# Attention and a gated feed-forward in one kernel: the softmax division moved behind the value product, the sigmoid made of exp and reciprocal, and the step order written anew

## The chip, the core and the metric

The kernel runs on one core of a Trainium2 chip. A core has a matrix engine (PE, with its weight loads shown as PEld), a vector engine (DVE), a scalar engine (ACT), a general engine (POOL) and a queue engine (SP) that issues most DMAs. Each engine takes its instructions in order; engines wait for each other by semaphores. The metric is the device time of one execution in microseconds.

## The reference

Attention of 4 batches, 8 heads, 768 positions and 64 features, in which a query sees only the keys that share its 6-bit hash; its output is the input of a gated feed-forward. All arrays are float32.

```python
q_bits = (np.einsum('bhsd,dk->bhsk', q, proj) > 0)     # same for k
mask = q_bucket[:, :, :, None] == k_bucket[:, :, None, :]
scores = np.where(mask, scale * np.matmul(q, k.transpose(0, 1, 3, 2)), -1e9)
attn = np.exp(scores - np.max(scores, axis=-1, keepdims=True))
attn = attn / (np.sum(attn, axis=-1, keepdims=True) + 1e-09)
x = np.matmul(attn, v)            # heads laid side by side: (4, 768, 512)
gate_pre = sum(conv_w[k] * xp[:, k:k + S, :] for k in range(5))   # causal
gate = 1.0 / (1.0 + np.exp(-gate_pre))
out = (gate * (x @ w_val)) @ w_out
```

## The kernel before

A *unit* is one batch and head (32 in all); a *tile* is 128 query rows of a unit, so a unit has six tiles and the program 192 steps `k`. In the words below, `r` is `k % 6`. Products that need float32 accuracy are made of float32r parts: a high part and a remainder, `aq`/`bq` for the queries, `ak`/`bk` for the keys, `xh`/`xl` for the attention output, `hh`/`hl` for the gated values, two halves of each weight.

The order of PE, ACT, DVE and POOL is the order in which the Python code issues instructions (`manual_schedule`); SP's is set by a scheduler. One step of the loop issues:

- `keep_transposed`: two ACT copies of a transposed tile from PSUM (`tp`) to `pt`;
- `maxima`, `factors`, `shifts`: DVE takes the row maximum `nm` of the scores, then two tiny operations give `gs` and `nb`;
- `row_sums`, `recip`, `normalise`: DVE adds 1e-9 to the row sums of two tiles, takes their reciprocal `ri`, and POOL multiplies each tile `p` (128x768) by it;
- `scores` of the next tile: four PE matmuls into `s` (two PSUM buffers, so tile k+2 waits for the exponential of tile k);
- `exponentials`: ACT makes `p` from `s` and sums its rows (`sm`);
- a step of `convs`: generator `pair_x`, which for each pair of heads makes `xh`, `xl` and the five-tap gate `g` (DVE, 128x768);
- steps of `weights`: converting the float64-stored weights, one every unit or so, until about the tenth unit;
- a step of `moes`: the feed-forward of a finished batch. A *chunk* is a value product (`val`) or an output product (`outp`), 12 matmuls cut into *thirds* of 4; a batch has 8 + 6 chunks. All of them accumulate in one PSUM buffer `m` until the loop is over;
- a step of `preps`: the parts `aq`, `bq`, `ak`, `bk` of the next unit, made with DVE, POOL and six SBUF-to-SBUF DMAs;
- two steps of `avs` on odd `k`: `attn_v`, the value product of a unit, six key blocks of four matmul records each into `av`;
- `transposes` of tile k-3 (`LAG = 3`): six PE transposes into `tp` (two buffers).

A value product ends with two ACT copies of `av` into `x`. When the last pair of a batch has its gate, ACT makes all four sigmoids, for which it loads another table and then the exponential's again; only then does the batch's feed-forward begin. Two output products of each batch but the last are held back until the next batch's feed-forward is there. After the loop, the rest of the feed-forward runs with five PSUM buffers.

## Time and profile before

| | us |
|---|---|
| median of three runs (637.18 to 638.35) | 637.83 |
| the profiled execution, its own time | 637.56 |
| its span in the trace | 635.6 |
| first row maximum starts | 11.5 |
| row maximum of step 48 starts (first batch done) | 148.1 |
| row maximum of step 191 (the last) starts | 575.7 |

The span falls into a head of 11.5 us, a first batch of steps 0 to 47 in which there is no feed-forward but the weights are converted, steps 48 to 191 in which the feed-forward of the batch before runs between the attention's matmuls, and a tail in which the last batch's feed-forward is left. In the rows of the profile, a busy PE is one that has a matmul in flight; how long a group of matmuls holds PE is read from the start of one group to the start of the next.

### The profile page before, as it was taken

Reading aid. Unit: us, or ns where it says so; the run is one execution under the profiler, and the core shown is the slowest. Engines: PE = TensorE matmul, PEld = TensorE weight load, DVE = VectorE, ACT = ScalarE, POOL = GpSimd, SP = SyncE. Lnnn points to the kernel's source line nnn. Section 1 sums busy time; section 2 is a strip of 40 time slices with the busy share of each in tenths; the row PEclk is TensorE's granted clock in tenths of the full one; section 3 lists DMA queues with packets and bytes.
Section 4 is the critical chain, followed back from the end, with each engine's and each line's share of the span. In section 5 each row is a group of like instructions: output and inputs, shape, how many; then the busy total and the mean of one; then the engine's idle time right before and its main releaser. Section 6 shows DMA issues by size and latency. Waiting matters only on the chain.

```text
span 635.6 us, 10630 instructions
## 1 busy us (share of the span) xinstructions
PE 590.1 (93%) x3496; PEld 424.3 (67%) x3496; DVE 465.9 (73%) x1064; ACT 421.7 (66%) x881; POOL 364.7 (57%) x326
## 2 busy tenths in 40 slices
PE   4689888878999999999999999999999999999997
PEld 2465554555567777676667877677667777776895
DVE  5789897999986766668675877578685787665532
ACT  3487776767778666667787766677778677675400
POOL 1375868577765764567653776466562677544221
PEclk9899998998999999999999999999999999999999
DMA  6533535443332334343433333343422223300111
GB/s 243 128 101 86 139 96 138 112 134 81 104 80 58 83 75 123 82 105 96 104 80 79 88 80 110 80 121 80 120 57 61 57 53 79 86 18 2 50 51 50
DMA packets 23269, 56.76 MB, mean 89 GB/s; under 512 B 4296, under 2 KB 4296, under 8 KB 23216
## 3 DMA queue, kind: packets, MB, share of 16 engines
q1 hardware_dynamic: 23072, 56.06, 32.9%
q8 instruction: 28, 0.46, 0.3%
q14 instruction: 25, 0.20, 0.1%
q10 hardware_dynamic: 144, 0.03, 0.0%
HBM read 23.12 MB, written 6.29 MB: 46 GB/s over the span
## 4 chain that ended last, share of the span: by engine, by line
PE 64%; DVE 18%; ACT 10%; issue 3%; DMA 3%; POOL 0%; DVEq 0%; ACTq 0%
PE av L303 16%; PE s L232 15%; PE tp L280 12%; PE m L390 8%; PE m L365 7%; DVE nm L238 6%; ACT p L256 4%; DVE g L334 3%; ACT pt L289 3%; ACT x L311 2%; DMA w<-in_w_out_dram 2%; DVE aq L166 1%; PE tp L365 1%; PE tp L390 1%; PE s L390 1%
## 5 line engine op out<-in xcount | busy, mean ns | idle before, releaser
L271 POOL TENSOR_SCALAR p<-p,ri 128x768 f32<-128x768 f32 x192 | 220.0, 1150 | 200.3 <-DVE nb L248 157.6
L256 ACT ACTIVATE p<-s,nb,gs 128x768 f32<-128x768 f32 x192 | 192.7, 1004 | 49.7 <-DVE nb L248 44.6
L289 ACT COPY pt<-tp 128x384 f32<-128x384 f32 x384 | 166.2, 485 | 86.0 <-PE tp L280 85.0
L238 DVE TENSOR_REDUCE nm<-s 128x1 f32<-128x768 f32 x192 | 182.4, 950 | 52.8 <-PE s L232 52.6
L280 PEld LDWEIGHTS tp<-ident,p 128*128 128x128 f32 x1152 | 130.4, 142 | 74.2 <-issue 47.3
L280 PE MATMUL tp<-ident,p 128*128 128x128 f32 x1152 | 165.4, 280 | 4.5 <-ACT pt L289 1.6
L232 PE MATMUL s<-ak,aq 76*128 76x384 f32 x384 | 118.6, 390 | 32.2 <-ACT p L256 25.4
L303 PE MATMUL av<-pt,vt 128*64 128x384 f32 x768 | 146.9, 504 | 0.0
L232 PE MATMUL s<-bk,bq 128*128 128x384 f32 x384 | 101.6, 346 | 0.0
L232 PEld LDWEIGHTS s<-ak,aq 76*128 76x128 f32 x384 | 59.4, 195 | 48.9 <-ACT p L256 39.3
L303 PEld LDWEIGHTS av<-pt,vt 128*64 128x64 f32 x768 | 47.4, 137 | 63.3 <-issue 62.7
L334 DVE SCALAR_TENSOR_TENSOR g<-x,cw_sb,g 128x768 f32<-128x768 f32 x64 | 78.4, 1225 | 0.2
L232 PEld LDWEIGHTS s<-bk,bq 128*128 128x128 f32 x384 | 71.9, 194 | 0.5 <-issue 0.5
L376 POOL TENSOR_TENSOR hl<-ht,hh 128x384 fp32r<-128x384 f32 x32 | 33.4, 1044 | 45.5 <-DVE hh L374 45.5
L168 POOL TENSOR_TENSOR bq<-r,aq 128x768 fp32r<-128x768 f32 x31 | 58.4, 1885 | 0.5 <-DVE aq L166 0.5
L311 ACT COPY x<-av 64x384 f32<-64x384 f32 x64 | 30.4, 475 | 33.5 <-PE av L303 32.9
L365 PE MATMUL m<-xh,wv 128*128 128x384 f32 x200 | 42.7, 337 | 0.0
L248 DVE TENSOR_SCALAR nb<-nm,gs 128x1 f32<-128x1 f32 x192 | 40.1, 209 | 3.5
L370 DVE TENSOR_TENSOR ht<-m,g 128x384 f32<-128x384 f32 x25 | 13.9, 555 | 35.4 <-PE m L365 32.0
L256 ACT ACTIVATION_READ_ACCUMULATOR p<-s,nb,gs 128x1 f32 x192 | 39.1, 204 | 0.0
L324 POOL TENSOR_TENSOR xl<-x,xh 128x384 fp32r<-128x384 f32 x32 | 33.5, 1066 | 9.5 <-DVE xh L323 9.5
L390 PE MATMUL m<-wo,hh 128*128 128x512 f32 x144 | 38.1, 394 | 0.0
(84 smaller groups left out, 475.6 us busy)
## 6 DMA issues: line engine op xcount, KB each, us to landing
r<-in_qk_dram SPq DMA_DIRECT2D x32, 384.0 KB
vt<-in_v_dram SPq DMA_DIRECT2D x16, 384.0 KB
out_dram<-o SPq DMA_DIRECT2D x24, 256.0 KB
ak<-aq SPq DMA_DIRECT2D x31, 192.0 KB
bk<-aq SPq DMA_DIRECT2D x31, 192.0 KB
bk<-bq SPq DMA_DIRECT2D x31, 192.0 KB
bq<-aq SPq DMA_DIRECT2D x31, 192.0 KB
w<-in_w_val_dram SPq DMA_DIRECT2D x4, 512.0 KB
```

Of the source, the lines that this page charges most:

```text
L168: nc.gpsimd.tensor_tensor(out=bq, in0=r, in1=aq.bitcast(FP32), op=ALU.subtract)
L232: nc.tensor.matmul(out=s[:, hf, 0:HS], lhsT=lq[0:n, qs], rhs=rk[0:n, hf * HS:(hf + 1) * HS], start=n == M, stop=n == P)
L238: nc.vector.tensor_reduce(out=nm, in_=s[:, :, 0:HS], axis=AX.XY, op=ALU.max, negate=True)
L256: nc.scalar.activation(out=p, in_=s[:, :, 0:HS], func=AF.Exp, bias=nb, scale=gs.pop(k), accum_out=sm[:, k % 2, 0:1])
L271: nc.gpsimd.tensor_scalar(out=p, in0=p, scalar1=rcs.pop(k), scalar2=1.0, op0=ALU.mult, op1=ALU.mult)
L280: nc.tensor.transpose(out=tp[:, n * P:(n + 1) * P], in_=p[:, kb * P:(kb + 1) * P], identity=ident)
L289: nc.scalar.copy(out=pt[:, :, qo:qo + P], in_=tp[:, 0:HS].rearrange("p (a b) -> p a b", b=P))
L303: nc.tensor.matmul(out=av[s * D:(s + 1) * D, 0:HS], lhsT=vt[:, kb, hh * D:(hh + 1) * D], rhs=pt[kb // 3][:, kb % 3, :], start=(kb == 0), s ...
L311: nc.scalar.copy(out=x[hh * D:(hh + 1) * D, o:o + HS], in_=av[s * D:(s + 1) * D, 0:HS])
L334: nc.vector.scalar_tensor_tensor(out=g, in0=x[:, k:k + S], scalar=w, in1=g, op0=ALU.mult, op1=ALU.add)
L365: nc.tensor.matmul(out=acc[:, 0:HS], lhsT=wv[wi][:, c, j * P:(j + 1) * P], rhs=xs_[(c, o)][xi], start=(m == 0), stop=(m == 11))
L390: nc.tensor.matmul(out=acc, lhsT=hs[(o, j)][hi][:, tb * P:(tb + 1) * P], rhs=wo[wi][:, j, :], start=(m == 0), stop=(m == 11))
```

## The change

The diff is cut to what sets the order and the costs.

```diff
-    LAG = 3
+    LAG = 1
...
+    rp = ctx.enter_context(tc.tile_pool(name="rp", bufs=2))
+    dp = ctx.enter_context(tc.tile_pool(name="dp", bufs=2, space=bass.MemoryType.DRAM))
...
-        nc.vector.tensor_copy(out=aq, in_=r)
+        nc.gpsimd.tensor_copy(out=aq, in_=r)
...
-    def normalise(k):
-        p, _ = ps[k]
-        nc.gpsimd.tensor_scalar(out=p, in0=p, scalar1=rcs.pop(k), scalar2=1.0, op0=ALU.mult, op1=ALU.mult)
+    def row_sums(i):
+        s1 = small.tile([P, KB], FP32, name="s1", bufs=2)
+        nc.vector.tensor_scalar(out=s1, in0=sms.pop(i), scalar1=1e-9, scalar2=None, op0=ALU.add)
+        ri = small.tile([P, KB], FP32, name="ri", bufs=2)
+        nc.vector.reciprocal(out=ri, in_=s1)
+        rows = dp.tile([2, P, KB // 2], FP32, name="rows")
+        nc.sync.dma_start(out=rows.rearrange("s p t -> p s t"), in_=ri.rearrange("p (s t) -> p s t", s=2))
+        return rows
+
+    def row_factors(i, rows):
+        rb = rbs[i] = rp.tile([P, P, KB // 2], FP32, name="rb")
+        for s in range(2):
+            nc.sync.dma_start(out=rb[s * D:(s + 1) * D], in_=rows[s].partition_broadcast(D))
...
+    def take(i, av):
...
-            nc.scalar.copy(out=x[hh * D:(hh + 1) * D, o:o + HS], in_=av[s * D:(s + 1) * D, 0:HS])
+            nc.vector.tensor_tensor(out=x[hh * D:(hh + 1) * D, o:o + HS].rearrange("d (t p) -> d t p", p=P),
+                                    in0=av[s * D:(s + 1) * D, 0:HS].rearrange("d (t p) -> d t p", p=P),
+                                    in1=rb[s * D:(s + 1) * D].rearrange("d p t -> d t p"), op=ALU.mult)
...
-            nc.vector.tensor_copy(out=xh, in_=x0)
+            nc.gpsimd.tensor_copy(out=xh, in_=x0)
...
+        if c == NP - 1:
+            moes.append(moe(b, xs_, gs))
...
-            for g in gs:
-                nc.scalar.activation(out=g, in_=g, func=AF.Sigmoid)
+        nc.scalar.activation(out=g, in_=g, func=AF.Exp, scale=-1.0)
+        yield
+        nc.gpsimd.tensor_scalar(out=g, in0=g, scalar1=1.0, scalar2=3.0e38, op0=ALU.add, op1=ALU.min)
+        yield
+        nc.vector.reciprocal(out=g, in_=g)
+        yield
...
-                nc.vector.tensor_copy(out=hh, in_=ht)
+                nc.gpsimd.tensor_copy(out=hh, in_=ht)
...
+            puts.append(lambda: put(o + tb * P, acc))
+        def put(r0, acc):
             ob = op.tile([P, 512], FP32, name="o")
-            if cur["gates"]:
-                nc.vector.tensor_copy(out=ob, in_=acc)
-            else:
-                nc.scalar.copy(out=ob, in_=acc)
+            nc.scalar.copy(out=ob, in_=acc)
...
+    def chunk_step(r):
+        if (cur["third"] or r in (0, 4)) and step(moes):
+            cur["third"] = (cur["third"] + 1) % 3
...
             if k < N:
                 exponentials(k)
-            if k >= 60 or k % 2:
+            drain(puts)
+            if r == 4:
+                drain(taken)
+            else:
                 step(convs)
...
+            if r == 0 or r == 2 or r == 4:
+                chunk_step(r)
             step(preps)
...
-            if k % 2:
-                step(avs)
-                step(avs)
+            if r == 1 or r == 3:
+                for _ in range(KB // 2):
+                    step(avs)
             if 0 <= k - LAG < N:
                 transposes(k - LAG)
+            if r == 2 or r == 4 or r == 5:
+                chunk_step(r)
```

So the value product of a unit runs in steps r = 1 and r = 3 of the next unit, three key blocks each; two chunks of the feed-forward run in a unit, one in r = 0 and 2, one in r = 4 and 5, with the thirds on both sides of the transposes in r = 2 and 4. The tiles `p` stay undivided: once a unit has its six row sums, their reciprocals go through DRAM to a tile `rb` that holds them in every partition, and `take` multiplies by it while it moves `av` to `x`. Each pair's gate gets its sigmoid as soon as it is made: exp on ACT, 1 + on POOL, reciprocal on DVE. The copies to `xh`, `hh` and `aq` go from DVE to POOL. A batch's feed-forward starts with its last pair's `xh`, not after its gates, and nothing is held back.

DVE, a stretch of two steps in a unit that has a pair's gate in hand. Before:

```order
L238 TENSOR_REDUCE nm_2179<-s_2146 128x1
L262 TENSOR_SCALAR s1_2181<-sm_2126 128x2
L244 TENSOR_SCALAR gs_2183<-nm_2179 128x1
L266 RECIPROCAL ri_2185<-s1_2181 128x2
L248 TENSOR_SCALAR nb_2188<-nm_2179,gs_2183 128x1
L238 TENSOR_REDUCE nm_2208<-s_2190 128x1
L244 TENSOR_SCALAR gs_2210<-nm_2208 128x1
L248 TENSOR_SCALAR nb_2213<-nm_2208,gs_2210 128x1
L166 CAST aq_2223<-r_1208 128x768
```

The same engine after, in steps r = 2, 3 and 4 of such a unit:

```order
L251 TENSOR_SCALAR nb_3664<-nm_3660,gs_3662 128x1
L356 RECIPROCAL g_3384<-g_3384 128x768
L241 TENSOR_REDUCE nm_3693<-s_3666 128x1
L247 TENSOR_SCALAR gs_3695<-nm_3693 128x1
L251 TENSOR_SCALAR nb_3697<-nm_3693,gs_3695 128x1
L241 TENSOR_REDUCE nm_3730<-s_3699 128x1
L247 TENSOR_SCALAR gs_3732<-nm_3730 128x1
L251 TENSOR_SCALAR nb_3734<-nm_3730,gs_3732 128x1
L323 TENSOR_TENSOR x_3524<-av_3641,rb_3630 64x384 x2
```

The tiny operations on row sums are gone from between the maxima, and a reciprocal of 768 elements in each partition stands ahead of the row maximum of r = 3.

PE, from the end of one output product to the first third of the next. Before:

```order
L390 MATMUL m_2908<-wo0_120,hl_2501 128x512
L390 MATMUL m_2908<-wo0_120,hl_2555 128x512
L390 MATMUL m_2908<-wo0_120,hl_2679 128x512
L390 MATMUL m_2908<-wo0_120,hl_2798 128x512
L280 MATMUL tp_3001<-ident_106,p_2864 128x128 x3
L280 MATMUL tp_3005<-ident_106,p_2864 128x128 x3
L232 MATMUL s_3020<-ak_2711,aq_2710 128x384 x2
L232 MATMUL s_3020<-bk_2713,bq_2712 128x384 x2
L390 MATMUL m_3027<-wo0_120,hh_2499 128x512
```

After, from r = 5 to r = 0:

```order
L409 MATMUL m_4430<-wo0_125,hl_3965 128x512
L409 MATMUL m_4430<-wo0_125,hl_4046 128x512
L409 MATMUL m_4430<-wo0_125,hl_4188 128x512
L409 MATMUL m_4430<-wo0_125,hl_4292 128x512
L235 MATMUL s_4500<-ak_4237,aq_4236 128x384 x2
L235 MATMUL s_4500<-bk_4239,bq_4238 128x384 x2
L409 MATMUL m_4512<-wo0_125,hh_3963 128x512
```

Between the last write to `m` and its next there were transposes and scores, and now there are scores alone; the copy that empties `m` stands on ACT behind the exponential of r = 0.

DVE behind the last value product. Before:

```order
L323 CAST xh_7467<-x_7423 128x384
L323 CAST xh_7471<-x_7423 128x384
L332 TENSOR_SCALAR g_7480<-x_7423,cw_sb_117 128x768
L334 SCALAR_TENSOR_TENSOR g_7480<-x_7423,cw_sb_117,g_7480 128x768 x4
L396 COPY o_7530<-s_7513 128x512
L370 TENSOR_TENSOR ht_7546<-tp_7533,g_6373 128x384
L374 CAST hh_7553<-ht_7546 128x384
L370 TENSOR_TENSOR ht_7565<-s_7548,g_6847 128x384
```

After:

```order
L323 TENSOR_TENSOR x_7097<-av_7174,rb_7170 64x384 x2
L356 RECIPROCAL g_6966<-g_6966 128x768
L347 TENSOR_SCALAR g_7209<-x_7097,cw_sb_122 128x768
L349 SCALAR_TENSOR_TENSOR g_7209<-x_7097,cw_sb_122,g_7209 128x768 x2
L389 TENSOR_TENSOR ht_7226<-m_7211,g_6087 128x384
L349 SCALAR_TENSOR_TENSOR g_7209<-x_7097,cw_sb_122,g_7209 128x768 x2
L389 TENSOR_TENSOR ht_7248<-tp_7229,g_6537 128x384
L356 RECIPROCAL g_7209<-g_7209 128x768
L389 TENSOR_TENSOR ht_7269<-s_7251,g_6966 128x384
L389 TENSOR_TENSOR ht_7288<-tp_7271,g_7209 128x384
```

The reciprocals of the last two pairs stand in this queue, one ahead of the last pair's taps and one ahead of the gated values of the last two columns.

## The prediction

> **What bounds the kernel now.** I read the page's busy line first, then the table of stages, then who PE waits for, then short stretches of the timeline. The stages' columns are stretch, length, and each engine's busy time with its count, then PE's granted clock, the DMA share and GB/s.

> ```profile
> PE 590.1 (93%) x3496; PEld 424.3 (67%) x3496; DVE 465.9 (73%) x1064; ACT 421.7 (66%) x881; POOL 364.7 (57%) x326
> 11.50:148.10 136.60, 115.35 (x677) 75.69 (x677) 119.96 (x272) 96.58 (x207) 90.02 (x77) 0.96 0.42 113
> 148.10:575.70 427.60, 416.44 (x2529) 302.62 (x2527) 312.74 (x744) 309.52 (x648) 256.30 (x227) 1.00 0.32 83
> 575.70:635.60 59.90, 54.77 (x282) 44.13 (x280) 26.74 (x43) 12.69 (x23) 15.61 (x15) 1.00 0.11 40
> PE s L232 <- ACT p L256: 8.1, 18, 2.1
> PE tp L280 <- DVE u L197: 1.6, 4, 0.4
> ```

> The first batch (stage 1) is bound by DVE, 120 of 136.6 us busy, with PE idle for 21. Stage 2, two thirds of the span, is bound by PE: its waits there (the last two rows) come to 9.7 us of 427.6. So a change that only relieves POOL, ACT or DVE can win little in stage 2, and any new wait of PE there adds to the time. The tail is one batch's feed-forward and what must be done before it.

> How long PE needs for each group is read between starts. Two steps without feed-forward, all engines:

> ```profile
> 302.28 0.86 ACT L289 COPY pt<-tp 128x384 f32<-128x384 f32 x2 [0.76 <-PE tp L280]
> 302.33 0.59 PE L232 MATMUL s<-ak,aq 76*128 76x384 f32 x2
> 303.04 1.01 ACT L256 ACTIVATE p<-s,nb,gs 128x768 f32<-128x768 f32 x1
> 303.11 0.82 PE L280 MATMUL tp<-ident,p 128*128 128x128 f32 x6
> 303.31 0.96 DVE L238 TENSOR_REDUCE nm<-s 128x1 f32<-128x768 f32 x1 [1.21 <-PE s L232]
> 304.01 0.87 ACT L289 COPY pt<-tp 128x384 f32<-128x384 f32 x2
> 304.18 0.62 PE L232 MATMUL s<-ak,aq 76*128 76x384 f32 x2 [0.25 <-ACT p L256]
> 304.50 0.21 DVE L248 TENSOR_SCALAR nb<-nm,gs 128x1 f32<-128x1 f32 x1
> 304.80 0.99 ACT L256 ACTIVATE p<-s,nb,gs 128x768 f32<-128x768 f32 x1
> 305.07 1.51 PE L303 MATMUL av<-pt,vt 128*64 128x384 f32 x8
> 306.52 0.87 PE L280 MATMUL tp<-ident,p 128*128 128x128 f32 x6
> 307.15 0.60 PE L232 MATMUL s<-ak,aq 76*128 76x384 f32 x2
> ```

> Scores hold PE for 0.78 us (302.33 to 303.11), or 0.89 ahead of a value product (304.18 to 305.07); transposes 0.63 (306.52 to 307.15). The row maximum starts 0.98 after its scores, the exponential 1.49 after the row maximum, the next ACT operation 0.97 after the exponential's start, and the scores of tile k+2 0.13 after its end. In a step with nothing but scores and transposes PE needs 1.41, ACT 1.73 (302.28 to 304.01), so PE idles.

> ```profile
> 193.72 1.56 PE L365 MATMUL m<-xh,wv 128*128 128x384 f32 x8
> 195.12 0.86 PE L365 MATMUL m<-xl,wv 128*128 128x384 f32 x4
> 195.90 1.51 PE L303 MATMUL av<-pt,vt 128*64 128x384 f32 x8
> 585.04 4.39 PE L303 MATMUL av<-pt,vt 128*64 128x384 f32 x24
> 589.36 2.11 PE L390 MATMUL m<-wo,hh 128*128 128x512 f32 x8
> 591.31 1.08 PE L390 MATMUL m<-wo,hl 128*128 128x512 f32 x4
> 592.23 1.99 PE L390 MATMUL tp<-wo,hh 128*128 128x512 f32 x8
> ```

> A value third costs 0.70 (two in 1.40 from 193.72), 0.78 ahead of a value product; six key blocks 4.32; an output third 0.92 (591.31 to 592.23).

> **The price that decides.** The one new operation of which the trace has no like is the reciprocal of 128x768 on DVE, 16 times. Rows for it and for the moved and removed operations:

> ```profile
> L266 DVE RECIPROCAL ri<-s x96: 165/166/167, 19.0 to 578.6; 128x2 f32<-128x2 f32 x96
> L262 DVE TENSOR_SCALAR s<-sm x96: 147/158/972, 18.8 to 578.3; 128x2 f32<-128x2 f32 x96
> L334 DVE SCALAR_TENSOR_TENSOR g<-x,cw_sb,g 128x768 f32<-128x768 f32 x64 | 78.4, 1225 | 0.2
> L332 DVE TENSOR_SCALAR g<-x,cw_sb 128x768 f32<-128x768 f32 x16 | 13.2, 827 | 0.0
> L166 DVE CAST aq<-r 128x768 fp32r<-128x768 f32 x31 | 20.6, 665 | 0.2
> L323 DVE CAST xh<-x 128x384 fp32r<-128x384 f32 x32 | 18.4, 596 | 10.8 <-ACT x L311 9.3
> L370 DVE TENSOR_TENSOR ht<-m,g 128x384 f32<-128x384 f32 x25 | 13.9, 555 | 35.4 <-PE m L365 32.0 <-ACT g L338 3.4
> L271 POOL TENSOR_SCALAR p<-p,ri 128x768 f32<-128x768 f32 x192 | 220.0, 1150 | 200.3 <-DVE nb L248 157.6 <-ACT x L311 12.0 <-PE tp L280 9.1
> L376 POOL TENSOR_TENSOR hl<-ht,hh 128x384 fp32r<-128x384 f32 x32 | 33.4, 1044 | 45.5 <-DVE hh L374 45.5
> L338 ACT ACTIVATE g<-g 128x768 f32<-128x768 f32 x16 | 12.2, 832 | 0.0
> L398 ACT COPY o<-m 128x512 f32<-128x512 f32 x12 | 7.0, 587 | 3.2 <-PE m L390 2.2
> ```

> From below: a one-pass operation on 128x768 takes 0.8 to 1.2 us (L332, L334), so about 0.9. From above: on two elements the reciprocal takes 166 ns, never more than 167, where an addition on the same shape takes 147 at least and 158 in the middle. If the 8 to 19 ns more belong to the elements, that is 4 to 9.5 ns for each beside some 1.3 of a pass (1.0 us over 768): 4 to 8 us for 768. I take the middle, 6.2 us, since the same instruction at a small shape is a nearer row than another instruction at this shape; a constant extra latency would explain the 8 ns as well, which is the first rival.
> [...]

> **The change part by part.**
> *Stage 1* (-5, then +10). DVE loses 9 casts of `aq` (9 x 0.665), 6 of `xh` (6 x 0.596) and 26 pairs of row-sum operations (26 x 0.32): 18 us. It gains 14 multiplications in `take` (14 x 0.56 by L370) and 7 small pairs: 10. Net -8; since units without gate work cannot go below what ACT and PE leave (four light steps of 1.73 and two of 0.89 + 2.16 + 0.63 make 14.3, where a unit now takes 136.6 / 8 = 17), I take -5. Two reciprocals fall here, 2 x 5.3 more than a pass, in a stage where DVE is the bound: +10.
> *Stage 2, the order* (+2). A unit with two value chunks holds PE for 4 x 0.78 + 2 x 0.89 + 6 x 0.63 + 4.32 + 6 x 0.70 = 17.2 us, its steps beginning at 0, 2.11, 5.79, 8.60, 12.28 and 15.09. One run of key blocks fewer in each of 24 units saves 24 x 0.11, thirds no longer ahead of value products 24 x 0.08, and all waits for ACT go, since every step now has PE work between a tile's transposes and the scores that wait for it: -2.6 - 1.9 - 9.7. Against it: an output product now inside the loop (2.8; before it was held for the tail); some 14 steps without feed-forward (unit 8 and the gaps between batches) at about 0.4 (5.6); and a new wait. Where an output product ends in r = 5, its copy out of `m` stands behind the exponential of r = 0: scores at 0, copy at 0.98 + 1.49 + 0.97 = 3.44, done at 4.03, while PE is at the next third at 0.78 + 0.63 + 0.92 + 0.78 = 3.11. That is 0.92 us, eight times: 7.4. Behind that third the transposes and everything else on PE queue.
> *Stage 2, the reciprocals* (+16). It is issued in r = 2 behind `nb`, whose row maximum starts at 2.11 + 0.98: at 4.5. At 6.2 us it ends at 10.7; the row maximum of r = 3, which could have started at 6.8, starts then, its exponential at 12.2, and the scores of r = 4 at 13.3 where PE is there at 12.28. So 1.0 us shows, because the value product of r = 3 covers the rest; 12 times, and some 4 us for unit 8, whose DVE still converts weights. Were that cover gone, all 4 us of lateness would show.
> *Tail* (-9, then +10). From the last row maximum: exponential done at 2.5, transposed 3.3, copied 4.2, value product 8.5, `take` (two of 0.56) 9.7, first value third 10.3 with the POOL cast at about 0.6 (between DVE's 0.60 for such a cast, L323, and POOL's 1.04, L376). Five value products (10.5) bring PE to 20.8. The first output product needs the last pair's gate: five taps, exp 0.83, POOL 1.15, reciprocal, product, split. With 0.9 for each reciprocal that is ready at about 23, with 6.2 at 33.5, since both last pairs' reciprocals stand in line. Then 22.9 of chunks and 4.7 of last split, copy and store: 51 or 61 against 59.9.
> *At no cost*: POOL loses 220 us (L271) and gains about 100 in casts and gate additions, busy 57% now; the exponential for the sigmoid costs ACT what the sigmoid did (L338) and spares table loads, which are on no path in stage 2 beside those waits; the three DMAs of `rb` start in r = 0 and 1 and are needed at 12.3, ten us later; SP passes them ahead of `prep`'s, which has the unit to spare. Without that cover `take` would stop DVE. The multiplication reads `rb` at a step of three words: at 0.56 I price it as if that were free.
> [...]

> **The sum.** -5 + 2 - 9 = -12 for all but the long reciprocal, and 10 + 16 + 10 = +36 for it: +24 on the profiled execution's 637.56 (span 635.6 and 2 around it), which is 0.3 below the median: 662.

> **Rivals.** *The reciprocal is one pass* (0.9 us): the terms of +36 go, 626, faster. For it: a fixed latency explains 166 against 158; against: 165 to 167 in 96 cases, above nearly all additions. The two cancel at a reciprocal of 0.9 + 5.3 x 12/36, about 2.7 us. [...] *The cover in r = 3 fails*, say because `ht` and `take` behind the reciprocal delay more: 2 us more in each of 12, 686. For it: after 10.7 DVE has 2.8 us of maxima, `ht` and `take` in 3.7; against: the waits computed for r = 4 and 5 have 0.6 in hand. *The factors come late*: `take` waits at the head of DVE with two dependent DMAs in front; 3 us in each of 24 units is 72, on top 734; it begins when they need over ten us.

> **How the numbers follow.** Forecast (4 to 8 us, cover holds) 0.68: its own range is 648 to 680, since 4 us would make the +36 to 21 and 8 us to 48, with some 5 for the rest; one pass 0.22; cover fails 0.07; factors late 0.03. Of the one-pass case I leave out its lower half, and above it the last two in part: 628 to 688. Faster by over 0.2% (about what a measurement of this kernel tells): the one-pass case less 0.02, and 0.02 of the forecast, 0.22; the same 0.04; slower 0.74.

> **What would show it.** The row of RECIPROCAL g at 128x768: 6 us for the forecast, 1 for the first rival. In stage 2, PE waits at scores for ACT behind it, about 1 us in every second unit, and at the first third of a product for ACT's copy, eight times. In the tail, PE waits for `hh` by some 12 us. If stage 1 is below 132 with the long reciprocal, my DVE count is wrong; if DVE waits for a DMA at `take`, the last rival is there.

## The result, and the profile after

| | before | after |
|---|---|---|
| median (range) | 638.09 (637.18 to 640.47) | 679.35 (677.69 to 681.94) |
| profiled execution, its own time | 637.56 | 681.94 |
| its span | 635.6 | 680.2 |
| head, up to the first row maximum | 11.5 | 11.6 |
| stage 1, steps 0 to 47 | 136.6 | 152.4 |
| stage 2, steps 48 to 191 | 427.6 | 453.4 |
| tail | 59.9 | 62.8 |

The change makes the kernel slower, 1.064 times (95% interval 1.060 to 1.069). The forecast was 662, the range 628 to 688 holds the result, and the forecast is 17 us short of it. The stages are read from one profiled execution each; the one after lies 2.6 us above its median. The loss of 44.6 us of span lies in all parts: 15.8 in stage 1, 25.8 in stage 2, 2.9 in the tail. The busy line of the page and the three stages after (same columns as before):

```profile
PE 602.9 (89%) x3496; PEld 442.5 (65%) x3496; DVE 527.0 (77%) x910; ACT 387.4 (57%) x821; POOL 255.5 (38%) x245
```

```profile
11.60:164.00 152.40, 124.87 (x694) 84.65 (x694) 132.65 (x245) 92.81 (x201) 55.50 (x48) 0.93 0.44 114
164.00:617.40 453.40, 425.49 (x2559) 317.02 (x2558) 365.47 (x635) 281.10 (x597) 172.15 (x166) 0.97 0.37 89
617.40:680.20 62.80, 49.07 (x234) 39.06 (x233) 22.52 (x23) 10.56 (x20) 21.80 (x22) 0.91 0.12 37
```

PE executes the same 3496 matmuls but is busy 12.8 us longer. The column behind the engines says why: the granted clock is 0.93, 0.97 and 0.91 in the three parts, where it was 0.96, 1.00 and 1.00. The second thing to see is who PE waits for in stage 2 (engine and line <- releaser: us in total, times, longest):

```profile
PE s L235 <- ACT p L260: 19.5, 15, 2.2
PE m L409 <- ACT o L418: 4.6, 5, 0.9
PE m L384 <- ACT o L418: 2.8, 3, 0.9
```

The first row was 8.1 us. The other two are the eight waits for a copy, 7.4 us. The prices of the new operations, from the groups by line and, for the two of the gate, one line of the program each (ns min/median/max, first and last start):

```profile
L323 DVE TENSOR_TENSOR x<-av,rb 64x384 f32<-64x384 f32 x64 | 43.0, 671 | 12.9 <-PE av L309 10.9
L269 DVE RECIPROCAL ri<-s 128x6 f32<-128x6 f32 x32 | 6.1, 191 | 1.1
L356 DVE RECIPROCAL g<-g x16: 4941/4952/4953, 90.6 to 643.7; 128x768 f32<-128x768 f32 x16
L354 POOL TENSOR_SCALAR g<-g x16: 2772/2773/2775, 87.8 to 640.9; 128x768 f32<-128x768 f32 x16
```

And who DVE waits for, over the whole span:

```profile
DVE g L356 <- POOL g L354: 21.3, 10, 3.3
```

The reciprocal takes 4.95 us. POOL's pass takes 2.77, not the 1.15 that I gave it, and ten of the sixteen reciprocals stand at the head of DVE's queue until it is done. One such place, in the timeline:

```profile
206.75 2.77 POOL L354 TENSOR_SCALAR g<-g 128x768 f32<-128x768 f32 x1
206.82 0.21 DVE L251 TENSOR_SCALAR nb<-nm,gs 128x1 f32<-128x1 f32 x1
209.56 4.95 DVE L356 RECIPROCAL g<-g 128x768 f32<-128x768 f32 x1 [2.52 <-POOL g L354]
213.97 0.87 PE L286 MATMUL tp<-ident,p 128*128 128x128 f32 x6
214.43 0.90 DVE L241 TENSOR_REDUCE nm<-s 128x1 f32<-128x768 f32 x1
215.86 0.99 ACT L260 ACTIVATE p<-s,nb,gs 128x768 f32<-128x768 f32 x1 [4.73 <-DVE nb L251]
216.99 0.44 PE L235 MATMUL s<-ak,aq 76*128 76x384 f32 x1 [2.15 <-ACT p L260]
218.94 1.48 PE L286 MATMUL tp<-ident,p 128*128 128x128 f32 x6
220.07 1.54 PE L384 MATMUL m<-xh,wv 128*128 128x384 f32 x4
```

DVE has done `nb` at 207.03, waits 2.52 for POOL, is held until 214.5, and the row maximum, the exponential and the scores follow late: PE stands 2.15 us. What comes behind it costs time as well: the transposes of 218.94 hold PE for 1.13 us, where they held it for 0.63 in the kernel before. The same place by stretches of 2 us; the granted clock is the third column from the end:

```profile
214.00:216.00 2.00, 0.84 (x8) 0.60 (x6) 1.93 (x5) 0.14 (x1) 0.00 (x0) 1.00 0.44 83
216.00:218.00 2.00, 1.01 (x6) 1.01 (x7) 1.90 (x5) 2.00 (x5) 1.51 (x2) 0.99 0.28 114
218.00:220.00 2.00, 2.00 (x10) 1.91 (x9) 1.90 (x4) 0.89 (x3) 1.63 (x3) 0.50 0.00 0
220.00:222.00 2.00, 2.00 (x14) 1.35 (x13) 0.33 (x2) 1.76 (x4) 1.92 (x3) 0.65 0.00 0
```

At this place PE begins to run at half clock (granted 0.50) 1 us after the stall ends, for 3.41 us. Five of the six stalls of this kind in stage 2 are followed by such a stretch, one is not. Added up over stretches of 1 us, length times missing clock is 11.9 us in stage 2 (before 1.7), 10.2 in stage 1 (before 5.1) and 5.8 in the tail (before none).

### The profile page after: what moved, and what is told of

It reads as the page before. It is cut to its first block, busy times and chain, and to the rows that moved or that the text cites. A ratio compares the mean times of both kernels' runs of the same rounds, so it can differ in the third digit from the quotient of the medians.

```text
span 680.2 us, 10112 instructions
## 1 busy us (share of the span) xinstructions
PE 602.9 (89%) x3496; PEld 442.5 (65%) x3496; DVE 527.0 (77%) x910; ACT 387.4 (57%) x821; POOL 255.5 (38%) x245
## 4 chain that ended last, share of the span: by engine, by line
PE 49%; DVE 30%; POOL 9%; ACT 6%; issue 5%; DMA 1%; DVEq 0%; ACTq 0%; POOLq 0%
PE s L235 13%; PE av L309 13%; PE tp L286 11%; DVE nm L241 8%; DVE g L356 7%; PE m L384 5%; PE m L409 5%; ACT p L260 4%; POOL g L354 4%; DVE g L349 3%; POOL hl L395 2%; POOL bq L170 2%; DVE nb L251 2%; DVE gs L247 1%; DVE x L323 1%
## 5 line engine op out<-in xcount | busy, mean ns | idle before, releaser
L286 PEld LDWEIGHTS tp<-ident,p 128*128 128x128 f32 x1152 | 138.2, 145 | 46.7 <-issue 33.3
L356 DVE RECIPROCAL g<-g 128x768 f32<-128x768 f32 x16 | 79.2, 4950 | 21.3 <-POOL g L354 21.3
L393 POOL CAST hh<-ht 128x384 fp32r<-128x384 f32 x32 | 23.4, 730 | 165.9 <-DVE ht L389 165.9
L349 DVE SCALAR_TENSOR_TENSOR g<-x,cw_sb,g 128x768 f32<-128x768 f32 x64 | 71.4, 1116 | 0.1
L354 POOL TENSOR_SCALAR g<-g 128x768 f32<-128x768 f32 x16 | 44.4, 2773 | 58.5 <-ACT g L352 57.9
L409 PE MATMUL m<-wo,hh 128*128 128x512 f32 x152 | 45.0, 416 | 13.2 <-POOL hh L393 7.9
L323 DVE TENSOR_TENSOR x<-av,rb 64x384 f32<-64x384 f32 x64 | 43.0, 671 | 12.9 <-PE av L309 10.9
L384 PE MATMUL m<-xh,wv 128*128 128x384 f32 x208 | 48.6, 359 | 3.5 <-ACT o L418 3.5
L337 POOL CAST xh<-x 128x384 fp32r<-128x384 f32 x32 | 16.9, 528 | 89.9 <-DVE x L323 89.9
L168 POOL CAST aq<-r 128x768 fp32r<-128x768 f32 x31 | 26.1, 843 | 57.8 <-PE s L235 43.3
```

The lines of the kernel that those rows point to most:

```text
L286: nc.tensor.transpose(out=tp[:, n * P:(n + 1) * P], in_=p[:, kb * P:(kb + 1) * P], identity=ident)
L349: nc.vector.scalar_tensor_tensor(out=g, in0=x[:, k:k + S], scalar=w, in1=g, op0=ALU.mult, op1=ALU.add)
L354: nc.gpsimd.tensor_scalar(out=g, in0=g, scalar1=1.0, scalar2=3.0e38, op0=ALU.add, op1=ALU.min)
L356: nc.vector.reciprocal(out=g, in_=g)
L384: nc.tensor.matmul(out=acc[:, 0:HS], lhsT=wv[wi][:, c, j * P:(j + 1) * P], rhs=xs_[(c, o)][xi], start=(m == 0), stop=(m == 11))
L409: nc.tensor.matmul(out=acc, lhsT=hs[(o, j)][hi][:, tb * P:(tb + 1) * P], rhs=wo[wi][:, j, :], start=(m == 0), stop=(m == 11))
```

## The experiments

The theory at the outset: the reciprocal in the row of the maxima makes the loss, with the stalls and the clock that it brings. The rivals: the new order of steps makes it (A), or POOL's long pass does (B). All kernels are the changed one with the edit shown, unless another base is named, and each ratio is to the kernel before, run anew beside them. For each, stages 1 and 2 of its profile (the same columns) carry the reading; stage 1 without the gate's long operations was 143.8 to 146.9 us in four profiles (without the reciprocal, without both, and two with tanh), so differences of 3 us there say nothing.

**Without the reciprocal.**

```diff
-        nc.vector.reciprocal(out=g, in_=g)
```

> The sixteen reciprocals of 128x768 are left out; the gate stays 1 + exp(-z), so what is computed is not the gate. The exponential and the POOL addition stay. Theory (the reciprocal in the row of the maxima, together with the stalls and clock losses it brings): -28 to -38 us in the two stages and -10 in the tail, so 632 to 642 us; the steps of 8.8 us fall to about 3.5. Rival A (the new order of steps and the waits for the copies carry most of the loss): no more than the 16 x 1 us that the engine itself is spared on the path, 660 us or more. Rival B (POOL's long addition, 2.77 us, carries it by holding up POOL's other work): 665 or more.

Measured: 643.12 (641.56 to 643.15), 1.0067 times before (1.0046 to 1.0088), a microsecond above the theory's range. Its stages 1 and 2:

```profile
11.40:158.30 146.90, 122.55 (x695) 80.50 (x694) 122.91 (x243) 92.04 (x201) 54.86 (x48) 0.94 0.46 118
158.30:587.30 429.00, 414.75 (x2559) 310.48 (x2558) 310.42 (x624) 279.94 (x597) 172.30 (x166) 1.00 0.39 94
```

Stage 2 is back at 429.0 with POOL's pass still there: rival B is out as a cause by itself, and rival A for stage 2.

**Without POOL's pass.**

```diff
-        nc.gpsimd.tensor_scalar(out=g, in0=g, scalar1=1.0, scalar2=3.0e38, op0=ALU.add, op1=ALU.min)
```

> The POOL pass (+1, then minimum) is left out; the reciprocal of the exponential itself is taken, so the gate is not the sigmoid. Theory: DVE no longer idles 2.5 us at the head of its queue for POOL; the steps of 8.8 us become about 6.3, the stall of PE behind them goes from 2.15 to below 0.5 us, and with it the half clock. Ten such waits of 2.1 us, some 8 us of clock loss and about 5 us in the tail: 645 to 655 us. Rival A (order): 672 to 680. Rival B (POOL): as low as with both left out.

Measured: 653.3 (650.94 to 655.03), 1.023 times (1.020 to 1.0261). Its stage 2:

```profile
160.90:593.60 432.70, 416.29 (x2558) 311.31 (x2557) 366.94 (x636) 281.54 (x597) 139.07 (x154) 0.99 0.38 93
```

The time lies in the theory's range. All twelve reciprocals of stage 2 are there, each 4.95 us, and the stage is 432.7.

**Without both.**

```diff
-        nc.gpsimd.tensor_scalar(out=g, in0=g, scalar1=1.0, scalar2=3.0e38, op0=ALU.add, op1=ALU.min)
...
-        nc.vector.reciprocal(out=g, in_=g)
```

> Both the POOL pass and the reciprocal are left out; the gate stays exp(-z). Theory: what is left is the new order with late division; my sum for that was 626 us, and the eight waits for a copy and the unpriced switches between thirds and scores are in it or add some 5: 626 to 636 us. Rival A: 655 or more, since the order stays as it is.

Measured: 641.74 (638.22 to 645.88), 1.0059 times (1.0025 to 1.0093). Its two stages and its tail:

```profile
11.50:158.40 146.90, 124.89 (x694) 85.38 (x694) 122.88 (x243) 92.93 (x201) 50.09 (x46) 0.93 0.46 118
158.40:587.10 428.70, 414.54 (x2559) 309.76 (x2557) 311.06 (x623) 280.21 (x597) 138.90 (x154) 1.00 0.39 94
587.10:639.20 52.10, 46.32 (x235) 37.84 (x233) 14.44 (x21) 10.61 (x20) 17.20 (x20) 1.00 0.14 45
```

This is above the 626 to 636 that I expected: the order alone is no gain but a loss of 0.6%. PE's waits for ACT's exponential in its stage 2:

```profile
PE s L235 <- ACT p L260: 5.0, 9, 1.8
```

The three runs together: in stage 2, POOL's pass alone costs 0.3 us (429.0 against 428.7), the reciprocal alone 4.0 (432.7), both together 24.7 (453.4). Neither is the cause by itself; 20 us belong to the pair, to a long operation that waits for its operand at the head of DVE's queue. By their size two readings add up to the 24.7: PE's waits for ACT are 14.5 longer (19.5 against 5.0) and the missing clock 10.2 (11.9 against 1.7). How much of the missing clock is lost time is the next question. In the tail (62.8; 54.0 with POOL's pass alone, 59.6 with the reciprocal alone, 52.1 with none) the pair costs 10.7. What remains after all is taken out is stage 1: 146.9, ten more than before, though no operation of the long gate is in it. Its missing clock is 10.2 us here, too, so what stage 1 loses by the clock over the kernel before (5.1) belongs to the order and not to the gate.

**The stall filled with work.** The transposes ahead of the stall are made four times into the same tiles (the second argument is how often):

```diff
-                transposes(k - LAG)
+                transposes(k - LAG, 4 if r == 3 and k >= 60 and k // KB % 4 == 2 else 1)
```

> In six units of stage 2 (each fourth, from the eleventh) the six transposes that stand ahead of the stall of 2.15 us are made four times instead of once, into the same tiles: 6 x 1.9 us more work for PE, all of it inside a stall. Nothing of the result changes. Theory (a stall of 2 us also makes PE run some 3.4 us at half clock soon after, five times in stage 2): the stall's length stays, the half clock goes, 5 x 1.7 = 8 us less: 669 to 674 us, and a granted clock in stage 2 of 0.99 instead of 0.97. Rival (the clock has another cause, or its loss is hidden): 679 to 683, or up to 690 if the added work is not hidden.

Measured: 675.33 (674.95 to 677.43), 1.0585 times (1.056 to 1.0609). The place of the timeline above, in this kernel, and its stage 2:

```profile
211.32 2.84 PE L286 MATMUL tp<-ident,p 128*128 128x128 f32 x24
214.34 0.62 PE L235 MATMUL s<-ak,aq 76*128 76x384 f32 x2 [0.18 <-ACT p L260]
215.84 0.82 PE L286 MATMUL tp<-ident,p 128*128 128x128 f32 x6
```

```profile
161.40:609.60 448.20, 429.73 (x2666) 323.20 (x2665) 367.27 (x636) 280.86 (x597) 172.39 (x166) 0.99 0.36 90
```

From the transposes to the scores it is 3.02 us in both kernels (213.97 to 216.99, 211.32 to 214.34), so the stall ends when it did. With 108 matmuls more, stage 2 is 5.2 us shorter, and its granted clock 0.99. The median is 4 us lower, 1.3 above the upper end of what I expected; the two intervals of the ratio just overlap, so the clock column is the better witness than the time. The missing clock of the stage falls from 11.9 us to 3.4 by stretches, its length by 5.2. Unit by unit, from one first row maximum to the next, the six units with a filled stall are 1.6, 1.0, 0.0, 0.8, 1.6 and 0.2 us shorter, and the 0.0 is the one whose stall had no slow stretch behind it. So the filling took away what the clock cost and nothing else: 5.2 of the 8.5 us of missing clock were lost time. Why a slow stretch cost 1.6 us in one unit and 0.2 in another is not shown. Of the 20 us of the pair, then, some 5 are the clock's, and the six stalls themselves are 12.8.

**The reciprocal one step later.**

```diff
         nc.gpsimd.tensor_scalar(out=g, in0=g, scalar1=1.0, scalar2=3.0e38, op0=ALU.add, op1=ALU.min)
         yield
+        yield
         nc.vector.reciprocal(out=g, in_=g)
```

> One step more lies between POOL's pass over the gate and DVE's reciprocal of it; the same operations, all of them. Theory (each of the two is free alone, and what costs is that the reciprocal, at the head of DVE's queue, waits 2.5 us for POOL): DVE no longer waits, the stall of 2.15 us and the half clock behind it go, and stage 2 takes the 433 us that it took without the POOL pass; stage 1 loses 3 us, the tail stays: 655 to 661 us. Rival (the reciprocal is covered only in r = 2, with the value product of r = 3 behind it; a step later it delays the row maximum of r = 4 in the open): 668 to 685.

Measured: 696.56 (695.68 to 698.77), 1.0907 times (1.0883 to 1.0932): slower than the changed kernel, and slower than the rival's own range. DVE's wait for POOL is 4.1 us, once; it cost more than it saved. PE's waits over the span, and stage 2:

```profile
PE s L235 <- ACT p L260: 25.2, 33, 2.9
PE av L195 <- DVE x L323: 15.3, 6, 3.6
PE s L235 <- POOL xh L337: 11.2, 5, 3.1
```

```profile
162.80:630.70 467.90, 429.28 (x2560) 320.71 (x2558) 371.84 (x636) 280.36 (x597) 172.52 (x166) 0.96 0.36 86
```

In r = 3 the reciprocal stands ahead of the row maximum and of `take` in r = 4. Then `x` comes late, POOL's cast of it holds up POOL's queue, and the matmuls that make the hash bits of a later unit (L195) wait for the PSUM tile `av`, which `take` has not yet emptied. I had counted the wait that goes and not what the new place is ahead of. The cover of the prediction (the value product of r = 3 hides a reciprocal issued in r = 2) is a property of that one place.

**The 1 added by ACT.** This keeps the reciprocal where it is and gives it its operand in time.

```diff
-        nc.gpsimd.tensor_scalar(out=g, in0=g, scalar1=1.0, scalar2=3.0e38, op0=ALU.add, op1=ALU.min)
+        nc.scalar.add(out=g, in_=g, add=1.0)
```

> The changed kernel with one edit: the 1 is added to the exponential by ACT (about 0.85 us, in the step after the exponential) and POOL's pass is gone; the minimum is left out, which changes nothing at these values. The reciprocal stays in r = 2 and is whole. Theory (the reciprocal costs little where its operand is ready when it reaches the head of DVE's queue; the loss came from its wait there): DVE's 21 us of waiting for POOL go, stage 2 takes 433 us and the whole 651 to 657. Rival (ACT's added pass in r = 1 delays the row's exponentials as POOL's delayed DVE): 665 to 680.

Measured: 656.02 (655.62 to 657.58), 1.0277 times (1.0255 to 1.0299). Its stage 2:

```profile
158.80:593.20 434.40, 416.94 (x2559) 311.41 (x2558) 369.52 (x636) 290.12 (x609) 139.18 (x154) 0.99 0.40 92
```

As expected (stage 2 was to take 433): the whole gate is computed, with 16 reciprocals of 4.95 us, and 23 us of the loss are gone.

**POOL's pass without the minimum.**

```diff
-        nc.gpsimd.tensor_scalar(out=g, in0=g, scalar1=1.0, scalar2=3.0e38, op0=ALU.add, op1=ALU.min)
+        nc.gpsimd.tensor_scalar(out=g, in0=g, scalar1=1.0, scalar2=None, op0=ALU.add)
```

> The changed kernel with POOL's pass over the gate cut to the addition; the minimum is left out, which changes nothing at these values. The pass took 2.77 us with an addition and a minimum, where the kernel before had 1.15 for two multiplications. Theory by dose: if the single addition takes 1.0 to 1.2 us, the reciprocal's wait shrinks from 2.5 to about 0.9 us, PE's stall from 2.15 to 0.6, too short for the half clock: 653 to 660. If the pass stays at 2.77 us: 677 to 682.

Measured: 665.59 (665.17 to 667.74), 1.0431 times (1.0402 to 1.0461). POOL's pass in its trace (one line of the program, ns min/median/max), and its stage 2:

```profile
L354 POOL TENSOR_SCALAR g<-g x16: 2125/2135/2139, 85.0 to 624.9; 128x768 f32<-128x768 f32 x16
```

```profile
159.90:601.40 441.50, 416.82 (x2559) 310.69 (x2557) 366.95 (x635) 280.85 (x597) 164.60 (x166) 1.00 0.39 91
```

Neither branch of what I had written: one addition takes 2.13 us, between the two. But the dose agrees. 0.64 us less in the pass shortens stage 2 by 11.9 us, with the granted clock back at 1.00: at the first of the six places DVE waits 1.77 us for POOL instead of 2.52, and the exponential 3.98 for `nb` instead of 4.73, so PE's stall of 2.15 there comes to an estimated 1.40 (2.15 less 0.75). Five slow stretches of 3.41 us at 0.50 would have left the stage's granted clock at 0.98.

**The gate from one operation.** A sigmoid is (1 + tanh(z/2))/2:

```diff
-        nc.scalar.activation(out=g, in_=g, func=AF.Exp, scale=-1.0)
-        yield
-        nc.gpsimd.tensor_scalar(out=g, in0=g, scalar1=1.0, scalar2=3.0e38, op0=ALU.add, op1=ALU.min)
-        yield
-        nc.vector.reciprocal(out=g, in_=g)
+        nc.scalar.activation(out=g, in_=g, func=AF.Tanh, scale=0.5)
...
-            late.append(lambda: nc.vector.tensor_tensor(out=ht, in0=acc[:, 0:HS], in1=g[j][:, o:o + HS], op=ALU.mult))
+            late.append(lambda: nc.vector.scalar_tensor_tensor(out=ht, in0=g[j][:, o:o + HS], scalar=1.0, in1=acc[:, 0:HS],
+                                                                 op0=ALU.add, op1=ALU.mult))
...
-            nc.scalar.copy(out=ob, in_=acc)
+            nc.scalar.mul(out=ob, in_=acc, mul=0.5)
```

> The gate is made of one ACT operation, tanh(z/2), in place of exponential, POOL pass and reciprocal; DVE's product becomes (t + 1) * value with the same count of instructions, and the factor 1/2 goes into ACT's copy of the output. Theory: the whole of what the reciprocal and its operand cost goes, so the time of the kernel with both left out, 642 us (638 to 646), the order alone still no gain over before. Rival (the exponential's and the tanh's tables are not loaded together, so ACT loads a table before and after each of 16 operations, in line with the row's exponential): 660 or more.

Measured: 640.29 (637.93 to 645.98), 1.0034 times (1.0003 to 1.0065), inside the theory's range. Two rows of ACT's groups:

```profile
L352 ACT ACTIVATE g<-g 128x768 f32<-128x768 f32 x16 | 13.4, 838 | 5.5 <-DVE g L349 5.5
L216 ACT ACT_TABLE_LOAD x1 | 1.3, 1283 | 1.2 <-PEq L573 1.2
```

One table load in the program, as in the changed kernel, where the kernel before had eight (7 for the sigmoid and back). So in this run the 192 exponentials of the rows and the 16 tanh had no load between them. The order alone still gains nothing.

**The copies first.** On top of the one before:

```diff
+            drain(puts)
             if k < N:
                 exponentials(k)
-            drain(puts)
```

> As the kernel with tanh, and the copies out of the output product's bank stand ahead of the step's exponential on ACT instead of behind it. Theory (PE waits ten times 0.9 us for these copies): 5 to 8 us less than with tanh alone, 633 to 637. Rival (the exponential then is late by the copy's 0.59 us and PE waits at the scores instead): within 3 us of tanh alone.

Measured: 633.76 (633.26 to 634.84), 0.9925 times (0.9906 to 0.9944). Stage 2 goes from 428.9 to 421.1, by 7.8, and both rows of PE's waits for the copy are gone from it. The late exponential costs nothing that shows: PE's waits for ACT's exponential are 5.0 us in stage 2 with and without the edit.

**Weight steps in r = 1 and 3.** On top of the one before:

```diff
-            for _ in range((1, 0, 2, 0, 2, 2)[k % 6]):
+            for _ in range((1, 2, 0, 2, 1, 1)[k % 6]):
```

> As the one before, and the steps of weight conversion stand mostly at r = 1 and 3, where PE has a run of value blocks, instead of r = 2, 4 and 5. The question is stage 1, which took 147 us without the gate's extra work where it took 136.6 before and where I had forecast 132. Theory (DVE's lumps of weight work and PE's runs of three key blocks fall into different steps, so each waits for the other in turn): stage 1 at 138 to 143, the total 4 to 8 us less than the one before. Rival (DVE's sum of work bounds stage 1): 146 to 148, the total unchanged.

Measured: 634.78 (631.67 to 641.34), 0.9937 times (0.9908 to 0.9966): no gain over the one before. Its profiled execution took 641.34, far above its median, and its stages are not used. By itself this says only that this place of the weight steps is no better.

What stage 1 waits for shows in the profile of the kernel with the copies first. The fifth unit, r = 4, in the timeline:

```profile
94.23 1.38 DVE L323 TENSOR_TENSOR x<-av,rb 64x384 f32<-64x384 f32 x2 [0.70 <-PE av L309]
95.64 1.20 DVE L94 TENSOR_SCALAR o<-o 128x512 f32<-128x512 f32 x1
96.64 0.59 PE L235 MATMUL s<-ak,aq 76*128 76x384 f32 x2 [0.28 <-POOL xl L338]
96.87 0.61 DVE L95 TENSOR_SCALAR o<-o 128x512 int32<-128x512 int32 x1
97.40 1.22 DVE L110 CAST wv<-w 128x512 fp32r<-128x512 f32 x1
98.65 0.96 DVE L241 TENSOR_REDUCE nm<-s 128x1 f32<-128x768 f32 x1
101.28 0.62 PE L235 MATMUL s<-ak,aq 76*128 76x384 f32 x2 [3.04 <-ACT p L260]
```

The two multiplications of `take` and three weight operations stand in line ahead of one row maximum, 4.4 us; PE's scores of the step after wait 3.04, and PE runs at half clock from 103 to 109 (0.50 in each stretch there). The units with taps are slow in another way: five taps stand in five steps of six there. The loop before the change stepped the gate in odd steps alone, so in stage 1 it had 10 taps (L332, L334); the changed kernel has 15 (L347, L349), those of one more pair. Here are the rows for four of each five, in stage 1, before and after:

```profile
L334 DVE SCALAR_TENSOR_TENSOR g<-x,cw_sb,g 128x768 f32<-128x768 f32 x8 | 10.2, 1272 | 0.0
L349 DVE SCALAR_TENSOR_TENSOR g<-x,cw_sb,g 128x768 f32<-128x768 f32 x12 | 14.2, 1188 | 0.0
```

**The taps one to an odd step, as before the change,** in stage 1 only, on top of the kernel with the copies first:

```diff
-            else:
+            elif k >= 48 or r % 2:
                 step(convs)
```

> The kernel with tanh and the copies first, and in the first batch (steps 0 to 47) the gate's taps again go one to every odd step, as in the kernel before, instead of five in a row in every second unit. Theory (stage 1 is longer than before because five taps of 1.16 us make the odd units DVE-bound at 17.9 us while the even ones wait for PE): odd units fall to 16 and even ones rise by at most 1, stage 1 at 141 to 144 against 146.7; total 628 to 631. Rival (the lump of take and weight steps in r = 4, with the half clock behind it, is what makes stage 1 long): stage 1 at 146 to 148, total 633 to 635.

Measured: 628.39 (626.38 to 632.16), 0.9847 times (0.9808 to 0.9886). Stage 1 takes 142.1 us. Both are what the theory gave, but not by its way: the units with taps do not fall to 16 us (17.0, 19.6 and 17.9; without the edit 17.9, 19.3 and 17.9), and the fifth unit falls from 21.1 to 16.4. The edit does two things at once: it spreads the taps, and stage 1 has 11 of them instead of 15.

**And no weight step in r = 4,** in stage 1, on top of the one before:

```diff
-            for _ in range((1, 0, 2, 0, 2, 2)[k % 6]):
+            for _ in range(((2, 1, 2, 1, 0, 1) if k < 48 else (1, 0, 2, 0, 2, 2))[r]):
```

> As the one before, and in the first batch no weight step stands in r = 4, where DVE has the two multiplications by the row factors; seven a unit as before, two each in r = 0 and 2, one each in r = 1, 3 and 5. Theory (both lumps matter): the steps of 6.5 us in the even units fall to about 4, PE's stalls of 3 us and the half clock behind them go: stage 1 at 135 to 141, total 622 to 629. Rival (the weight conversion's place does not matter, since DVE's sum of work sets the stage): as e11 within 2 us.

Measured: 616.73 (615.8 to 617.89), 0.9658 times before (0.9637 to 0.9679): the best of all, and faster than the kernel before. Stage 1 of the three, in their order (copies first; taps apart; no weight step in r = 4), each from its own profile:

```profile
11.50:158.20 146.70, 124.64 (x695) 83.28 (x695) 122.50 (x244) 92.89 (x201) 49.39 (x46) 0.90 0.48 118
```

```profile
11.50:153.60 142.10, 120.46 (x692) 78.35 (x692) 117.27 (x240) 91.93 (x201) 49.61 (x46) 0.95 0.51 122
```

```profile
11.50:142.40 130.90, 115.36 (x690) 77.21 (x689) 113.18 (x239) 90.97 (x198) 46.90 (x46) 0.97 0.54 131
```

In the last two, four taps of the first batch move behind step 48, which takes 5 us of DVE's work out of stage 1 and makes stage 2 no longer (420.3 and 421.6 against 421.1). Stage 1 itself becomes 15.8 us shorter; PE's waits for ACT there go from 15.4 to 11.7 us, the longest from 3.0 to 1.8, and the granted clock from 0.90 to 0.97. The place of the weight steps alone, with the same 11 taps, is worth 11.2 us (142.1 against 130.9), more than I gave it, and this excludes that DVE's sum of work sets the stage. The taps' edit is worth 4.6, little over the 3 us by which this stage differs between like kernels, and how much of it is the spreading and how much the four taps that moved is not shown.

## Why the prediction came out as it did

The sign and the range were right, and so was the cause in kind: the long reciprocal in DVE's queue. The size was not, and two of the six terms carry the miss, stage 1's order (15.3 us off) and stage 2's reciprocals (8.7 off). The order by itself, which I had at -12, came out at +3.6: not the gain that I forecast. Measured terms come from the kernel with neither operation (for the order) and from the changed kernel less that one (for the gate):

| term | forecast | measured |
|---|---|---|
| stage 1, order | -5 | +10.3 (146.9 against 136.6) |
| stage 2, order | +2 | +1.1 (428.7 against 427.6) |
| tail, order | -9 | -7.8 (52.1 against 59.9) |
| stage 1, reciprocals | +10 | +5.5 (152.4 against 146.9) |
| stage 2, reciprocals | +16 | +24.7 (453.4 against 428.7) |
| tail, reciprocals | +10 | +10.7 (62.8 against 52.1) |
| sum | +24 | +44.5 |

- *The price of the reciprocal*: 6.2 forecast (4 to 8), 4.95 measured. Against one pass, about 0.9, the row of 166 ns leaned the right way by 8 ns. The new row of six elements gives it closer: 191 ns against 166 for two is 6.25 ns an element, and 762 elements more make 191 + 4763 = 4954 ns.
- *The cover in r = 3* was computed rightly. With its operand in time, a reciprocal costs stage 2 4.0 us in all. The forecast let 1.0 us show at 6.2; DVE was in fact held 2.52 + 4.95 = 7.47 us at such a place, which by the same working lets 2.3 show, and 2.15 were measured. This happened in six of the twelve places; in the other six POOL's pass was done in time, but for 0.58 us once.
- *The step that failed in stage 2* is the cost of POOL's pass, 1.15 taken from L271 and 2.77 measured. I put it into the tail's chain alone. In the six places with a stall the pass starts 0.09 us after `bq` ends on POOL, and the reciprocal waits for it at DVE's head. That order could be followed before the run, and I did not follow that queue.
- *What was not in the sum at all* is PE's clock. The missing clock grows by 10.2 us in stage 2, of which the filled stalls gave back 5.2 in time, and by 5.1 in stage 1, where it is as large without the gate's operations. The stages of the profile before showed 0.96, 1.00 and 1.00; the 0.96 was there to be asked about.
- *The step that failed in stage 1* is -5 from a count of DVE's work, in two ways. The count left out the five taps, some 5.6 us (four of 1.19 and one of 0.81), that the new loop brings into stage 1: it gave 8 us less of DVE's work, and without the gate's long operations DVE is busy 2.9 us more there (122.88 against 119.96). And the stage is not bound by the sum: with the same 11 taps, the place of the weight steps made 142.1 or 130.9 us. That 130.9 lies near what the forecast would give (136.6 - 5 = 131.6) is no proof of the count, since four of the five taps are out of the stage again there.
- *Stage 2's order* is near by luck. I had all waits for ACT gone, and 5.0 us of the 8.1 are left; what made up for them is not shown.
- *The eight waits for a copy*, 0.92 us each, 7.4 in all: 4.6 + 2.8 measured, and 7.8 came back when the copies went first.
- *The factors* were never late: `take` waits for PE's `av` (10.9 of 12.9 us), no DMA. It takes 0.67 us where I had 0.56; how much of the 0.11 comes from reading `rb` at a step of three words is not shown.
- *In the tail*, PE's waits for `hh` are 8.5 us where I wrote 12. Its +10 is near the 10.7 in part by luck: with the reciprocal alone the tail is 7.5 us longer than with neither, and the rest came with POOL's pass.
- *The rivals*: the one pass is excluded by the row. That the cover fails is what happened in about half of the places, through POOL and not through `ht` or `take`; its 686 lies 7 us above the result, where my 662 lies 17 below. I gave it 0.07.

What stays open: why POOL needs 2.77 us for an addition and a minimum, 2.13 for an addition and 1.15 for two multiplications of the same shape (the multiplications also took one factor from a tile, where the others have constants); and how much idle time in a grid interval brings the half clock.

## What to carry to other kernels

A long operation in an in-order queue is free or dear by two things: whether its operand is there when it reaches the head, and what stands behind it at that place. Price the producer, too, and its own queue; here either operation alone cost 0.3 or 4 us of stage 2, and the pair 24.7. And when a stall of PE of 2 us is forecast, add what the clock may take behind it (here 5.2 us behind five stalls), and ask before an order is judged whether its lumps can be spread: the same order of the feed-forward, with the gate from one ACT operation, the copies first, and the first batch's DVE work spread and four of its taps moved on, is 3.4% faster than the kernel before.

## What the hardware showed that I had not expected

- In the changed kernel's profile, stalls of 2.13 to 2.15 us were followed by 3.41 us of PE at half clock (granted clock 0.50) where 1.84 us or more of the stall fell into one interval of a fixed grid of 3.41 us; the one that the grid parted into 0.87 and 1.26 us was not. The slow stretch began between 0.1 us ahead of the stall's end and 1.6 us behind it. With the stalls filled with repeated transposes the granted clock of stage 2 was 0.99 instead of 0.97, and 108 matmuls more took 5.2 us less.
- POOL's pass over 128x768 took 1.15 us with two multiplications, 2.13 with an addition and 2.77 with an addition and a minimum, the last two within 0.02 us over all sixteen.
- DVE's reciprocal took 166 ns at 2 elements of a partition, 191 at 6 and 4.95 us at 768, the last within 0.02 us in all sixteen: 6.25 ns for each element more.
